# A fused attention and two-layer gate kernel: the first four layer steps in two halves of 256 tokens

## The chip, the cores and the metric

The kernel runs on one core of one Trainium2 chip. The metric is the device time of one launch in microseconds (us); lower is better. Before the change the median of three runs is 987.04 us (983.0 to 988.54). TensorE does the matrix products, VectorE, ScalarE and POOL (GpSimd) the elementwise work, and SP issues the DMAs.

## What is computed

A gated linear attention over 4 batches of 8 heads, 768 positions, head size 48, then two layers on the 3072 tokens of 384 features, with a hidden width of 2048:

```
for t in range(S):
    state = alpha[:, :, t, :, None] * state + einsum('bhd,bhe->bhde', k[:, :, t], v[:, :, t])
    y[:, :, t] = einsum('bhd,bhde->bhe', q[:, :, t], state)
x = y as (3072, 384)
h = x @ w_in;  P = a0 + a1 h + a2 h^2 + a3 h^3;  Q = 1 + |b0||h| + |b1| h^2
x = (P / (Q + 1e-6)) @ w_out
h = x @ w2_in;  out = (h * tanh(softplus(h))) @ w2_out
```

The layer weights come as float64. All matrix products of the layers keep more than float32r precision: each operand is split into a high and a low part.

## The kernel before, in words

The positions are cut into six blocks of 128; a block holds 4 x 128 = 512 tokens. The attention of a block (`attend`) is two units (`attn_unit`), unit 0 for batches 0 and 1, unit 1 for batches 2 and 3; unit `b` yields 256 tokens. A unit is a chain: scores (line 449), six levels of a tree (line 482), transposes of K (line 546), the state's outer products (line 561), the outputs (lines 596, 632), and for blocks 0 and 1 their transposes (line 546 again) with copies on ScalarE into `xf` (line 657).

The layers are 12 phases (`PHASES`: layer, block) of 16 steps, one step for each 128 hidden features, 192 steps in all. A step has nine hidden matmuls (`hidden_mms`, line 673: three input slices by the three products high x high, high x low, low x high) of 128x512 into one of three PSUM banks, the gate (`hidden`: lines 688 to 706 for the first layer, a Mish at line 710 for the second), a split of the gate's result into high and low part (`split_g`, through the helpers at lines 226/228 and 219/221), and nine output matmuls (`out_mms`, line 722) that add into three further banks over the whole phase. The first layer's gate is five ScalarE instructions, three or four on VectorE, and one multiplication on POOL for some blocks. The input of a phase is split into `xh` and `xl` by `split_x` (cast at line 226 or 228, subtraction on VectorE at line 667). In the first phase of each layer `load_w` turns the float64 weights into high and low parts on ScalarE and VectorE (lines 340 to 369).

The order on each engine is set ahead of time. Every piece of work is put into a `Plan` with an engine, a cost, a due time, and what it reads and writes; `Plan.order` runs a list scheduler, the ready piece with the earliest due time first, and emits all instructions in that order. Due times come from `T_PH` (one number for each phase, times 16 steps), `LAG`, `D_MID`, `D_SPL`, and for the attention from `AT_P*` and `AT_W`. Letters in strings such as `E_GH`, `E_TREE`, `E_GL1` choose an engine by block (V VectorE, A ScalarE, P POOL). VectorE instructions that read PSUM are entered with `port=False`; the others and POOL's exclude each other in the plan. Until the first full layer step the plan fills TensorE's free time with warm-up matmuls (line 766) of 128x256 that compute nothing; each is two pieces in the trace.

The attention of block 0 uses the PSUM pair `bank[0]`, `bank[1]` for unit 0 and banks 2 and 3 for unit 1; block 1 uses the pair for both. The main loop before, at a phase's start:

```
split_x(l, V[i] - D_X)
if l == 0 and c < NBLK - 1:
    attend(c + 1)
```

## Time and profile before

| | |
|---|---|
| runs | 983.0, 987.04, 988.54 us; median 987.04 |
| profiled execution | 989.03 us, span of its instructions 987.2 us |
| mean granted TensorE clock | 0.997 of full speed |
| busy share | TensorE 97%, VectorE 69%, ScalarE 62%, POOL 22% |

A busy share is a mean over stages; the table of stretches shows them apart. Idle time of an engine is split by what ended it ("<- DVE zp L699": a VectorE instruction of line 699 that wrote zp). PEld is TensorE's weight load, which overlaps its matmuls. A matmul's duration in the trace overlaps the next one's; the distance of two starts is what it takes.

### The profile page before, as it was taken

To read this page: it belongs to the slowest core of one execution; us is meant where nothing else is said; L and a number is where in the kernel's file an instruction comes from. 1 tells how busy PE (TensorE), PEld (TensorE's weight loads), DVE (VectorE), ACT (ScalarE), POOL (GpSimd) and SP (SyncE) were. 2 spreads that over 40 slices of the span, in tenths; PEclk is the share of its full clock that TensorE was granted. 3 is DMA by queue.
4 is the path that set the end of the run, shared out by engine and by line. 5 is a ranking of instruction groups with operands and counts; after the bars stand their busy time and mean duration, and the time that the engine had idled before them with its cause. 6 is when DMAs were issued, how large, how long until landed. Compare 5 with 4: busy or idle time off the path is not lost.

```text
span 987.2 us, 24492 instructions
## 1 busy us (share of the span) xinstructions
PE 957.1 (97%) x10370; PEld 779.8 (79%) x10370; DVE 680.8 (69%) x907; ACT 610.4 (62%) x1042; POOL 219.5 (22%) x172
## 2 busy tenths in 40 slices
PE   7988998999999999999999999999999999999998
PEld 6776876778878888888878778888888878888886
DVE  5879899989999999927796985449921288611100
ACT  2787989799966688621488633457721398723422
POOL 2034575534200000233323200000023200000232
PEclk9999999999999999999999999999999999999999
DMA  7474848774688898469636856465565555565531
GB/s 307 137 258 195 277 134 304 248 242 145 238 325 311 277 326 288 139 203 309 220 85 210 280 201 205 124 190 148 146 207 155 154 156 148 164 191 145 162 105 46
DMA packets 75757, 199.99 MB, mean 203 GB/s; under 512 B 8192, under 2 KB 34944, under 8 KB 74112
## 3 DMA queue, kind: packets, MB, share of 16 engines
q1 hardware_dynamic: 75648, 198.43, 61.8%
q8 instruction: 81, 1.33, 0.5%
q14 instruction: 28, 0.23, 0.1%
...
## 4 chain that ended last, share of the span: by engine, by line
PE 69%; DVE 8%; ACT 4%; DMA 2%; issue 1%; POOL 0%; DVEq 0%; SPq 0%
PE bank L722 33%; PE bank L673 31%; PE pair L482 3%; DVE zp L706 1%; PE pair L632 1%; DMA qka<-in_qka_dram 1%; DVE zp L697 1%; DVE zp L699 1%; DMA stage<-in_w2o_dram 1%; PE pair L546 1%; PE pair L561 1%; ACT zp L701 1%; DVE stage L345 1%; DVE qka L497 1%; ACT u L688 1%
## 5 line engine op out<-in xcount | busy, mean ns | idle before, releaser
L722 PE MATMUL bank<-gg,wo 128*128 128x512 f32 x1728 | 428.1, 393 | 1.4 <-DVE wo L219 0.7
L722 PEld LDWEIGHTS bank<-gg,wo 128*128 128x128 f32 x1728 | 322.1, 188 | 69.6 <-DVE wo L219 1.1
L673 PE MATMUL bank<-xh,wih 128*128 128x512 f32 x576 | 229.3, 398 | 3.0 <-DVE zp L699 2.5
L673 PE MATMUL bank<-xl,wih 128*128 128x512 f32 x576 | 225.2, 391 | 1.3 <-DVE xl L667 1.3
L673 PE MATMUL bank<-xh,wl 128*128 128x512 f32 x576 | 225.0, 391 | 0.0
L221 POOL TENSOR_TENSOR gg<-zp,gg 128x512 fp32r<-128x512 f32 x64 | 92.2, 1441 | 399.9 <-DVE gg L228 205.4
L710 ACT ACTIVATE zp<-bank 128x512 f32<-128x512 f32 x96 | 57.2, 597 | 168.6 <-PE bank L673 151.9
L219 DVE TENSOR_TENSOR gg<-zp,gg 128x512 fp32r<-128x512 f32 x128 | 89.3, 703 | 71.7 <-ACT gg L226 71.3
L673 PEld LDWEIGHTS bank<-xh,wih 128*128 128x128 f32 x576 | 108.3, 188 | 27.4 <-DVE zp L699 3.9
L673 PEld LDWEIGHTS bank<-xl,wih 128*128 128x128 f32 x576 | 108.4, 188 | 23.3 <-DVE xl L667 2.0
L673 PEld LDWEIGHTS bank<-xh,wl 128*128 128x128 f32 x576 | 108.3, 188 | 22.8
L226 ACT CAST gg<-zp 128x512 fp32r<-128x512 f32 x144 | 89.4, 621 | 59.4 <-PE bank L722 42.2
L695 POOL TENSOR_TENSOR zp<-zp,u 128x512 f32<-128x512 f32 x48 | 70.1, 1463 | 111.3 <-ACT zp L694 111.1
L701 ACT ACTIVATE zp<-zp,c 128x512 f32<-128x512 f32 x96 | 69.5, 726 | 13.7 <-DVE zp L691 7.5
L697 DVE SCALAR_TENSOR_TENSOR zp<-zp,sc,bank 128x512 f32<-128x512 f32 x96 | 71.0, 742 | 9.3 <-ACT zp L696 8.9
L688 ACT ACTIVATE u<-bank 128x512 f32<-128x512 f32 x96 | 57.2, 596 | 27.0 <-PE bank L673 24.0
L699 DVE SCALAR_TENSOR_TENSOR zp<-zp,sc,bank 128x512 f32<-128x512 f32 x96 | 71.3, 744 | 2.9 <-ACT u L688 1.3
L570 POOL TENSOR_TENSOR tmp<-X,qk 48x768 f32<-48x768 f32 x16 | 26.1, 1629 | 197.5 <-DVE X L575 148.0
L696 ACT ACTIVATE zp<-bank,sc 128x512 f32<-128x512 f32 x96 | 66.4, 691 | 4.6 <-PE bank L673 4.5
L706 DVE SCALAR_TENSOR_TENSOR zp<-zp,sc 128x512 f32<-128x512 f32 x80 | 63.9, 804 | 7.4 <-ACT zp L705 5.6
L482 PEld LDWEIGHTS pair<-qka 48*64 48x64 f32 (+4 forms) x3200 | 45.1, 126 | 28.5 <-issue 10.6
L733 DVE COPY u<-bank 128x512 f32<-128x512 f32 x12 | 8.3, 692 | 82.9 <-PE bank L722 82.9
...
## 6 DMA issues: line engine op xcount, KB each, us to landing
wo<-woD SPq DMA_DIRECT2D x160, 384.0 KB, 3.3
wl<-wlD SPq DMA_DIRECT2D x160, 192.0 KB, 2.5
...
```

Source lines behind the costliest of these rows:

```text
L219: dve(n, due, reads, writes, lambda: nc.vector.tensor_tensor(**kw()))
L221: pool(n, due, reads, writes, lambda: nc.gpsimd.tensor_tensor(**kw()))
L226: act(n, due, reads, writes, lambda: nc.scalar.copy(out=out(), in_=in_()), src="s")
L482: nc.tensor.matmul(bk[j][o:o + m, lo + 32 * g:lo + 32 * (g + 1)].rearrange("p (n l) -> p n l", l=L), lhsT=K[h, e * HC:e * HC + m], rhs=Qv[ ...
L673: nc.tensor.matmul(bank[hb], lhsT=w[:, k * P:(k + 1) * P], rhs=x[k], start=(k == 0 and j == 0), stop=(k == KT - 1 and j == 2))
L688: act(NTOK, due, [kh, "tab"], [ku], lambda: nc.scalar.activation(u, h, AF.Abs), table="ln")
L695: pool(NTOK, due, [ku], [kz], lambda: nc.gpsimd.tensor_tensor(out=zs[r], in0=zs[r], in1=u, op=ALU.mult))
L697: dve(NTOK, due, [kh], [kp], lambda: nc.vector.scalar_tensor_tensor(out=ps[r], in0=ps[r], scalar=A2, in1=h, op0=ALU.add, op1=ALU.mult), po ...
L699: dve(NTOK, due, [kh], [kp], lambda: nc.vector.scalar_tensor_tensor(out=ps[r], in0=ps[r], scalar=A1, in1=h, op0=ALU.add, op1=ALU.mult), po ...
L701: act(NTOK, due, [], [kz], lambda: nc.scalar.activation(zs[r], zs[r], AF.Ln, bias=c_1), src="s", ptr=1, table="ln")
L706: dve(NTOK, due, [kw], [kp], lambda: nc.vector.scalar_tensor_tensor(out=ps[r], in0=ps[r], scalar=A0, in1=w(), op0=ALU.add, op1=ALU.mult), ...
L722: nc.tensor.matmul(bank[5 + k], lhsT=wos[b][:, w, k * P:(k + 1) * P], rhs=x[q], start=(f == 0 and j == 0), stop=(f == FT - 1 and j == 2))
```

## The change

The first four steps of the first phase are made in two halves of 256 tokens, as 128x256 matmuls. The first half (`h = 0`) needs unit 0's tokens alone; its hidden products go to the pair's banks and its gate buffers lie in `xf` and `q1`, which nothing else uses then. The second half uses the usual buffers. The order in the program is first halves, then `attend(1)`, then second halves. The input of the first phase is not copied to `xf`: ScalarE rounds it from PSUM to `xh`, and VectorE subtracts from PSUM to `xl`. Further: the gate's cast in the first phase moves from ScalarE to VectorE (`E_GH`); Mish results of blocks 1, 4 and 5 stay in their PSUM bank, from where they are split (`R_MISH`); the tree of block 5 and a product of block 4 go from VectorE to POOL; all due times have new values, with an offset for each weight load (`Q_CV`) and each half step (`Q_H`, `Q_HO`). The new letters B and C of the weight conversion are not used in `E_CV`, and the strings `E_YC`, `E_XH`, `E_KC` say ScalarE throughout.

```diff
-E_GH = ('AAAAVA', 'AVAVAA')
+E_GH = ('VAAAVA', 'AVVAAA')
-T_PH = (8.402, 4.739, 4.796, 8.179, 6.234, 8.56, 2.241, 9.509, 5.286, 22.879, 7.86, 1.937)
+T_PH = (10.073, 5.514, 5.295, 4.65, 6.569, 12.843, 1.516, 12.633, 0.776, 22.477, 6.651, 4.257)
-AT_W = ((-0.128, 67.387), (21.099, 31.988), (11.236, 69.526))
+AT_W = ((-6.443, 95.112), (37.494, 62.046), (-0.915, 14.198))
+NH = 4
+Q_H = (-1.546, -3.174, 20.938, 9.585, -64.563, -53.758, 42.057, -18.307)
+Q_HO = (-21.147, -10.271)
+HB = (0, 1)
-E_TREE = 'PPPVVV'
-E_QK = 'VVVVVV'
+E_TREE = 'PPPVVP'
+E_QK = 'VVVVPV'
-E_GL1 = 'VPVPVP'
+E_GL1 = 'VPVPPV'
+R_MISH = '.G..GG'
...
-        pe(0.6, now(), [kv], kB, lambda: transposes(vn, KT), 0.5)
+        for ds in ((0,), (1,)) if c == 0 else ((0, 1),):
+            pe(0.3 * len(ds), now(), [kv] + [kv + "ab"[d] for d in ds], [kB[d] for d in ds], lambda ds=ds: rows(ds), 0.5)
...
+                evict(E_XH[b][d], DM, now(), [kB[d]], ["xhb" + x], lambda t=t, y=y: xha[:, :, t], lambda y=y: y)
+                dve(DM, now(), [kB[d], "xhb" + x], ["xlb" + x], lambda t=t, y=y: nc.vector.tensor_tensor(
+                    out=xla[:, :, t], in0=y, in1=xha[:, :, t].bitcast(F32), op=ALU.subtract), port=False)
...
+    def gate_bufs(r, j, h2):
+        if h2:
+            n = NTOK if h2 == 2 else NTOK // 2
+            return zs[r][:, 0:n], ps[r][:, 0:n], us[j][:, 0:n], ""
+        n = NTOK // 2
+        t = [x[:, y * n:(y + 1) * n] for x in (xf.rearrange("p k t -> p (k t)"), q1.rearrange("p a d -> p (a d)")) for y in range(6)]
+        return t[r], t[NZ + r], t[2 * NZ + j], "h"
...
-            act(NTOK, due, [kh] + ([] if last else ["tab"]), [kp] + (["tab"] if last else []),
-                lambda: nc.scalar.activation(ps[r], h, AF.Mish), table="mish")
+            ko, o = (kh, h) if R_MISH[c] == "G" else (kp, pr)
+            act(n, due, [kh] + ([] if last else ["tab"]), [ko] + (["tab"] if last else []),
+                lambda: nc.scalar.activation(o, h, AF.Mish), table="mish")
...
+        if in_bank:
+            dve(n, due, [kp, kgh], [kgl], lambda: nc.vector.tensor_tensor(
+                out=gl, in0=g, in1=gh.bitcast(F32), op=ALU.subtract), port=False)
...
+        n, cs = (NTOK, slice(0, NTOK)) if h == 2 else (NTOK // 2, slice(h * NTOK // 2, (h + 1) * NTOK // 2))
+
         def mms(k):
             for j, (w, x) in enumerate(((0, ghs), (0, gls), (1, ghs))):
-                nc.tensor.matmul(bank[5 + k], lhsT=wos[b][:, w, k * P:(k + 1) * P], rhs=x[q],
-                                 start=(f == 0 and j == 0), stop=(f == FT - 1 and j == 2))
+                nc.tensor.matmul(bank[5 + k][:, cs], lhsT=wos[b][:, w, k * P:(k + 1) * P], rhs=x[q][:, 0:n],
+                                 start=(f == 0 and j == 0 and h != 1), stop=(f == FT - 1 and j == 2), skip_group_check=open_)
...
+    def step(i, hb, a, b, t, to, h=2):
+        l, _, f = steps[i]
+        r, q = count[0] % NZ, count[0] % NG
+        hidden_mms(hb, l, f, a, t, h)
+        count[0] += 1
+        hidden(l, hb, r, i, t + D_MID, h)
+        split_g(l, r, q, hb, i, t + D_MID + D_SPL[l], h)
+        out_mms(f, q, b, to, h, i < FT)
+
+    def half_step(i, h):
+        a, b = slots[i - i % 2]
+        t = V[i] + Q_H[h * NH + i]
+        step(i, HB[i % 2] if h == 0 else 2 + i % 2, a + i % 2, b + i % 2, t, t + LAG[0] + Q_HO[h], h)
...
-            split_x(l, V[i] - D_X)
-            if l == 0 and c < NBLK - 1:
+            if i:
+                split_x(l, V[i] - D_X)
+            if i == 0:
+                for h in range(2):
+                    for g in range(NH):
+                        half_step(g, h)
+                    if h == 0:
+                        hand_over(lent)
+                        attend(1)
+            elif l == 0 and c < NBLK - 1:
                 attend(c + 1)
```

The order of TensorE behind unit 0's output transposes (`pair<-cst,vn`), before. L365/L366 make low parts of weights, L766 is warm-up, `bank<-cst,zp` are the K transposes of unit 1:

```order
L546 MATMUL pair<-cst,vn_141 128x128 x6
L365 MATMUL bank_125<-stage,cst 128x384
L366 MATMUL bank_125<-wih_2_73,minus 128x384
L766 MATMUL bank_124<-cst 128x256 x3
L546 MATMUL bank_122<-cst,zp 128x128 x4
L546 MATMUL bank_123<-cst,zp 128x128 x4
L766 MATMUL bank_124<-cst 128x256 x4
```

And with the change (lines 390/391, 571, 684, 714 and 838 are what 365/366, 546, 546, 673 and 766 were):

```order
L684 MATMUL pair<-cst,vn_137 128x128 x6
L390 MATMUL bank_123<-stage,cst 128x384
L391 MATMUL bank_123<-wih_2_73,minus 128x384
L714 MATMUL pair<-xh,wih_0_71 128x256
L714 MATMUL pair<-xl,wih_0_71 128x256
L714 MATMUL pair<-xh,wl_87 128x256
```

Hidden matmuls of half width (128x256) stand where warm-up stood; twelve more like the last three rows follow before unit 1's K transposes.

The order of TensorE at unit 1's output transposes (`bank<-cst,u`), before, where the row of 128x512 is the first of the layers; `pair<-qka` is attention block 1:

```order
L766 MATMUL bank_124<-cst 128x256
L482 MATMUL pair<-qka_140 64x32 x32
L546 MATMUL bank_122<-cst,u 128x128 x3
L546 MATMUL bank_123<-cst,u 128x128 x3
L766 MATMUL bank_124<-cst 128x256 x5
L482 MATMUL pair<-qka_140 60x32 x32
L673 MATMUL bank_122<-xh_102,wih_0_71 128x512
L673 MATMUL bank_122<-xl_105,wih_0_71 128x512
L673 MATMUL bank_122<-xh_102,wl_87 128x512
```

With the change, where L794 is an output matmul (722 before) and L474 (449 before) is the first of attention block 1:

```order
L794 MATMUL bank_122<-gg,wo_91 128x256 x3
L794 MATMUL bank_123<-gg,wo_91 128x256 x3
L838 MATMUL bank_120<-cst 128x256
L684 MATMUL bank_118<-cst,u 128x128 x3
L684 MATMUL bank_119<-cst,u 128x128 x3
L838 MATMUL bank_120<-cst 128x256
L474 MATMUL pair<-qka_136 64x64 x32
L714 MATMUL bank_118<-xh,wih_0_71 128x256
L714 MATMUL bank_118<-xl,wih_0_71 128x256
L714 MATMUL bank_118<-xh,wl_87 128x256
```

Output matmuls of first halves stand ahead of unit 1's transposes, and block 1's attention has moved behind them.

The order of VectorE around unit 1's state (`X_137`), before; L228 with `xh` and L667 make the first input:

```order
L575 TENSOR_TENSOR X_137<-tmp,bank_122 48x8x48
L575 TENSOR_TENSOR X_137<-tmp,bank_123 48x8x48
L517 COPY_PREDICATED AT_139<-cst,pair 128x512
L491 TENSOR_TENSOR qka_140<-qka_140 128x1024
L219 TENSOR_TENSOR wo_94<-stage,wo_94 128x2x384
L357 SCALAR_TENSOR_TENSOR stage<-stage 128x768
L517 COPY_PREDICATED AT_139<-cst,pair 128x256x2
L497 TENSOR_TENSOR qka_140<-qka_140 128x2x256x2
L228 CAST xh_102<-xf 128x512
L228 CAST xh_103<-xf 128x512
L667 TENSOR_TENSOR xl_105<-xf,xh_102 128x512
L667 TENSOR_TENSOR xl_106<-xf,xh_103 128x512
```

With the change, from unit 0's input on (L696); L748, L750 and L759 are the gate (697, 699, 706 before), L600 is the state, L382, L243 and L234 are weights (357, 228, 219):

```order
L696 TENSOR_TENSOR xl<-pair,xh 128x3x128 x2
L748 SCALAR_TENSOR_TENSOR xf<-xf,sc,pair 128x256
L750 SCALAR_TENSOR_TENSOR xf<-xf,sc,pair 128x256
L382 SCALAR_TENSOR_TENSOR stage<-stage 128x768
L243 CAST wo_94<-stage 128x2x384
L234 TENSOR_TENSOR wo_94<-stage,wo_94 128x2x384
L759 SCALAR_TENSOR_TENSOR xf<-xf,sc,pair 128x256
L748 SCALAR_TENSOR_TENSOR xf<-xf,sc,pair 128x256
L243 CAST gg<-xf 128x256
L750 SCALAR_TENSOR_TENSOR xf<-xf,sc,pair 128x256
L759 SCALAR_TENSOR_TENSOR xf<-xf,sc,pair 128x256
L243 CAST gg<-xf 128x256
```

Gate instructions of the first halves now stand ahead of unit 1's state, and block 1's work (L517, L491, L497) is no longer there.

## Rows read from the trace of the kernel before

**Rows 1.** Page, part 1: busy us (share of the span) and instructions, TensorE.
```profile
PE 957.1 (97%) x10370; PEld 779.8 (79%) x10370; DVE 680.8 (69%) x907; ACT 610.4 (62%) x1042; POOL 219.5 (22%) x172
```

**Rows 2.** Busy us of each engine (instructions) by stretch; granted clock, DMA share, GB/s.
```profile
54.43:77.98 23.55, 20.44 (x481) 16.86 (x479) 16.60 (x21) 17.95 (x29) 9.11 (x8) 1.00 0.82 289
77.98:100.00 22.02, 18.73 (x259) 14.66 (x257) 20.36 (x23) 17.16 (x31) 11.07 (x7) 0.92 0.42 158
100.00:160.00 60.00, 58.65 (x912) 46.93 (x911) 54.54 (x59) 55.76 (x92) 37.45 (x29) 1.00 0.64 219
160.00:205.00 45.00, 41.03 (x654) 31.91 (x653) 42.66 (x52) 37.81 (x76) 23.05 (x18) 1.00 0.78 268
205.00:500.00 295.00, 294.10 (x3219) 239.30 (x3218) 256.56 (x340) 197.63 (x339) 64.04 (x45) 1.00 0.74 248
500.00:600.00 100.00, 96.29 (x1253) 78.41 (x1244) 83.88 (x111) 66.78 (x117) 22.55 (x17) 1.00 0.64 209
600.00:983.60 383.60, 381.87 (x2461) 315.08 (x2459) 167.16 (x255) 188.01 (x315) 43.05 (x33) 1.00 0.51 150
```

**Rows 3.** The same view for line 766 alone, the warm-up matmuls.
```profile
54.43:77.98 23.55, 9.93 (x40) 7.19 (x40) 1.00 0.82 289
```

**Rows 4.** Timeline of TensorE at 793 us: start, us, what, [idle before <- releaser].
```profile
793.55 0.51 PE L673 MATMUL bank<-xh,wih 128*128 128x512 f32 x1 [1.51 <-DVE zp L699]
```

**Rows 5.** Timeline of TensorE at 92 us.
```profile
92.13 0.76 PE L482 MATMUL pair<-qka 48*32 48x32 f32 x64 [1.96 <-DVE zp L706]
92.81 3.35 PE L722 MATMUL bank<-gg,wo 128*128 128x512 f32 x9
95.96 0.63 PE L673 MATMUL bank<-xh,wih 128*128 128x512 f32 x1
96.39 0.63 PE L673 MATMUL bank<-xl,wih 128*128 128x512 f32 x1
```

**Rows 6.** Chain that ended last, at 387 us: start, us, what.
```profile
386.96 2.04 PE bank L722 x9
```

**Rows 7.** Timeline of TensorE, 62 to 79 us.
```profile
62.30 1.12 PE L449 MATMUL pair<-qka 48*64 48x64 f32 x63
...
75.58 0.97 PE L482 MATMUL pair<-qka 48*60 48x32 f32 x54
...
77.98 0.50 PE L673 MATMUL bank<-xh,wih 128*128 128x512 f32 x1
```

**Rows 8.** Groups by line and shape, ScalarE: count | busy us, mean ns | idle before.
```profile
L688 ACT ACTIVATE u<-bank 128x512 f32<-128x512 f32 x96 | 57.2, 596 | 27.0 <-PE bank L673 24.0 <-DMA out_dram<-u 1.1 <-DVE zp L697 1.0
...
L694 ACT ACTIVATE zp<-u,sc 128x512 f32<-128x512 f32 x48 | 39.0, 817 | 0.1
```

**Rows 9.** Timeline of ScalarE, 70 to 74 us.
```profile
71.02 0.86 ACT L653 COPY u<-bank 128x384 f32<-128x384 f32 x2 [2.42 <-PE bank L596]
...
73.31 0.86 ACT L657 COPY xf<-bank 128x384 f32<-128x384 f32 x2
```

**Rows 10.** Timeline of VectorE at 170 us.
```profile
170.39 1.89 DVE L667 TENSOR_TENSOR xl<-xf,xh 128x512 fp32r<-128x512 f32 x3
```

**Rows 11.** Groups by line and shape, VectorE.
```profile
L219 DVE TENSOR_TENSOR gg<-zp,gg 128x512 fp32r<-128x512 f32 x128 | 89.3, 703 | 71.7 <-ACT gg L226 71.3
...
L228 DVE CAST gg<-zp 128x512 fp32r<-128x512 f32 x48 | 20.7, 433 | 60.8 <-ACT zp L710 51.7 <-PE bank L722 8.9
```

**Rows 12.** Timeline of TensorE, 200 to 210 us.
```profile
203.22 1.09 PE L546 MATMUL pair<-cst,qka 128*128 128x128 f32 x8
204.07 0.47 PE L673 MATMUL bank<-xh,wih 128*128 128x512 f32 x1
```

**Rows 13.** Groups by line and shape, TensorE weight loads.
```profile
L673 PEld LDWEIGHTS bank<-xl,wih 128*128 128x128 f32 x576 | 108.4, 188 | 23.3 <-DVE xl L667 2.0
```

**Rows 14.** TensorE's waits, 500 to 600 us: us in total, times, longest.
```profile
PE bank L673 <- DVE xl L667: 1.3, 1, 1.3
PE bank L673 <- DVE zp L699: 1.0, 1, 1.0
```

More of the change, by code (lines that the diff above doesn't have):

```diff
@@ L204, in pe @@
     def pe(us, due, reads, writes, emit, rows=1.0):
-        plan.add("PE", us if us == 0.680 else us + 0.2, due, reads, writes, emit, after=rows)
+        plan.add("PE", us if us in (0.680, 0.360) else us + 0.2, due, reads, writes, emit, after=rows)
     def dve(n, due, reads, writes, emit, port=True, fast=False, ptr=0):
@@ L214, in pool, with evict @@
         plan.add("POOL", 0.15 + (0.0021 if n > 2 * P else 0.00254) * n, due, reads, writes, emit, True)
+    def evict(eng, n, due, reads, writes, out, in_):
+        if eng == "A":
+            act(n, due, reads, writes, lambda: nc.scalar.copy(out=out(), in_=in_()))
+        else:
+            dve(n, due, reads, writes, lambda: nc.vector.tensor_copy(out=out(), in_=in_()), port=False)
     def tt(eng, n, due, reads, writes, kw):
@@ L679, in hidden @@
-    def hidden(l, hb, r, i, due):
+            pe(0.680 if h == 2 else 0.360, due, [f"wih{l}_{f // 2}", f"wl{a}"] + [f"xh{k}", f"xl{k}"] + xb, [f"bank{hb}"], lambda k=k: mms(k))
+    def gate_bufs(r, j, h2):
[5 more added lines that the diff above has]
+        return t[r], t[NZ + r], t[2 * NZ + j], "h"
@@ new lines, in hidden @@
+            kw = kh if R_PSUM[c] in "RG" else kz
+            w = lambda: h if R_PSUM[c] in "RG" else zr
+            ko = kh if R_PSUM[c] == "G" else kp
+            o = lambda: h if R_PSUM[c] == "G" else pr
+            act(n, due, [kz], [kw] + (["tab"] if last else []),
+                lambda: nc.scalar.activation(w(), zr, AF.Exp, scale=-1.0), src="s", table="ln")
+            dve(n, due, [kw, kp], [ko], lambda: nc.vector.scalar_tensor_tensor(
+                out=o(), in0=pr, scalar=A0, in1=w(), op0=ALU.add, op1=ALU.mult), port=R_PSUM[c] not in "RG", ptr=1)
+        else:
+            ko, o = (kh, h) if R_MISH[c] == "G" else (kp, pr)
+            act(n, due, [kh] + ([] if last else ["tab"]), [ko] + (["tab"] if last else []),
+                lambda: nc.scalar.activation(o, h, AF.Mish), table="mish")
```

143 lines of the change are left out of this document (88 added, 55 removed).

## Prediction

> **What bounds the kernel now.** I read the page's busy shares first, then busy times by stage, then TensorE's timeline and waits in the stages that are not full. TensorE is busy 97% of the span [rows 1], so the time is TensorE's useful work plus what it loses. From 205 us to 500 us it idles 0.9 us in 295 [rows 2]: there nothing is to be won. The losses lie in three places. From 54.43 to 77.98 us (the first attention unit, "unit 0", is through and the second, "unit 1", is not) it idles 3.1 us, and 9.9 us of its busy time are warm-up matmuls that compute nothing [rows 2, 3]. From 77.98 to 100 us, the pipe's first fill, it idles 3.3 us, and from 100 to 205 us 5.3 us [rows 2]. From 500 to 600 us it idles 3.7 us, and a wait of 1.5 us stands at 793 us [rows 2, 4]. A loss that is not idle time: from 92.81 us, after an idle of 1.96 us, nine output matmuls took 3.15 us up to the next start where nine take 2.04 us elsewhere, and the three hidden ones behind them start 0.43 us apart instead of 2.04 / 9 = 0.227 [rows 5, 6]; the granted clock of that stage is 0.92 on average [rows 2]. That is 1.1 + 3 x 0.2 = 1.7 us. VectorE stands close behind: 91% busy from 100 to 160 us, 95% from 160 to 205 us [rows 2].
>
> **The change part by part.** All sums start from the profiled execution: 989.03 us, of which 987.2 us are span; that is 2.0 us above the median of the three runs, 987.04 us, and I carry the difference over to the median.
>
> *Half steps in place of warm-up.* In the new order 54 half matmuls (36 hidden, 18 output) stand ahead of unit 1's transposes, and 7 warm-up matmuls instead of 20 stand behind unit 0's. Useful work brought forward: 54 halves are 27 full ones at 0.227 us, 6.1 us. The 13 warm-up matmuls that go are 13 x 9.93 / 20 = 6.5 us (each is two of the 40 pieces of [rows 3]), so there is room for it without a later start. On the other side, four TensorE groups of attention block 1 began before the first layer matmul at 77.98 us, from 62.30 to 75.58 us (the first and the last of the four are in [rows 7]); now one does. Three groups of about 1.12 us, 3.4 us, come later. Net 2.7 us won.
>
> *Unit 1's chain and its input.* ScalarE gets 20 half-width activations of the first half's gates, and they stand between the copies of unit 1 that TensorE waits for: three ahead of its K copies, five ahead of its state copies, the rest ahead of its output copies. Half of the shortest and of the longest of the full-width ones is 0.30 and 0.41 us [rows 8]; I take 0.35. The first eight make unit 1 some 3 us late; the rest fall for the most part into the 2.42 us that ScalarE waited for TensorE before 71.02 us [rows 9]. Ends 0 and 5. Against this the input is rounded from PSUM: before, from the copies into xf to the first matmul it took 77.98 - 73.31 = 4.7 us [rows 7, 9], with rounding and subtraction on VectorE in between; now two casts and two subtractions of 384 columns, about 2.0 us: the two copies of that width took 0.86 us, and a subtraction of 512 columns 0.63 us in a row of three, so 0.55 us each is on the safe side [rows 9, 10]. That gives 2.7 us back. Net 0.3 us lost, taken as 0: the second halves start near 78 us, as the first full steps did.
>
> *The fill, 78 to 100 us.* Outputs of the first halves are then ready while the second halves are still in the gates, so TensorE has work where it waited: 3.3 us of idle and 1.7 us of low clock. I take 3.5 of these 5.0 us; ends 0 and 5.0. From 100 to 205 us I take 1.3 of 5.3 us, for VectorE sets the pace there.
>
> *VectorE's load.* E_GH moves the cast of the first phase from ScalarE to VectorE: 16 x 0.43 us (the casts' mean [rows 11]), 6.9 us more, in a stretch where VectorE is 91 to 95% busy. Up to the last input subtraction of block 1 the new VectorE order holds 31 gate instructions more, 24 of the new ones of half width, some 8 us at 0.2 to 0.7 us each by the same rows, and four weight conversions more; TensorE's order is then 1.33 groups of nine further, 2.7 us. VectorE idled 14.1 us from 54.43 to 160 us [rows 2], which covers it if half of that can be used. I charge 2.0 us; ends 0 and 8.
>
> *Halves cost more than wholes.* 144 half matmuls stand for 72 full ones. No row shows 256 columns in this format. Below: exactly half, 0.113 us, no cost. Above: no gain from the narrower operand, 0.227 us, 16.3 us. The nearest row: eight 128-column transposes with the same 128x128 float32 weights follow each other in 0.85 us, 0.106 us each [rows 12], so the array takes new weights at least that fast, though a single load reads 188 ns [rows 13]. I take 0.12 us: 144 x 0.12 - 16.3 = 0.9 us lost. The Trainium skill, "TensorE: Matmul & The Clock Gate", section "LDWEIGHTS (loading the stationary operand)", has a load of 128 columns take 128 / 1.2 = 107 ns however wide the moving operand is, which at 256 columns is as long as the matmul itself. By that rule an estimate of 144 x 0.109 us gives a gain of 0.6 us instead of the loss, and the row of 0.106 us agrees with it better than the one of 188 ns does.
>
> *Later parts.* Block 4's attention is due over 95 us instead of 67, block 5's over 62 instead of 32 (AT_W), and one product of block 4 and the tree of block 5 go to POOL, which is 23% busy there. The idle of 500 to 600 us and the wait at 793 us end mostly on VectorE instructions [rows 14], an engine that is 84% busy from 500 to 600 us [rows 2]; spread thinner, I take half of 3.7 + 1.5 us, 2.6 us; ends 0 and 5.2. Mish results that stay in PSUM (blocks 1, 4, 5) move 32 subtractions from POOL to VectorE at 0.70 us each [rows 11]: 11 us of block 1's come between 205 and 500 us, where VectorE has 38 us of room and covers them, the others behind 600 us, where it is 44% busy [rows 2]. I cost it at nothing; without that cover it would be up to 11 us.
>
> Sum: 2.7 + 0 + 3.5 + 1.3 - 2.0 - 0.9 + 2.6 = 7.2 us. 989.0 - 7.2 = 981.8 us for the profiled execution, 987.0 - 7.2 = **979.8 us** for the median.
>
> **The rivals.**
> *All waits go.* The whole of 5.0, 5.3 and 5.2 us is recovered and neither VectorE nor the halves cost: 2.7 + 5.0 + 5.3 + 5.2 = 18.2, 969 us. For it: the idle before 205 us has many small causes that one order can avoid. Against: VectorE at 95%.
> *VectorE gives it back.* The 6.9 us of casts and the earlier gates meet a VectorE that has no room, and the 2.7 + 3.5 + 1.3 us shrink to 2 while the late 2.6 us stay away: with the halves' 0.9 us, 986 us. For it: 91 to 95% busy. Against: its 8.6 us of idle from 54.43 to 100 us fall in the stretch that gets the new work [rows 2].
> *Weight loads set the halves' pace.* At 0.188 us per half matmul [rows 13], 90 of the 144 (those that do not stand in place of warm-up) cost 0.075 us more each, 6.8 us: 979.8 + 6.8 = 986.6 us. For it: the row. Against: the 0.106 us of the transposes.
> *The clock falls.* With 12 fewer warm-up matmuls in all, the thin stretch of 55 to 78 us may fall to the lower of TensorE's levels (1.2 against 2.4 GHz). Each stretch like that at 92.81 us costs 1.7 us; two of them make it 983.2 us. The Trainium skill, "TensorE: Matmul & The Clock Gate", section "HAM oscillation — how this bites in real kernels", warns that idle gaps bring the lower clock back; by that rule taking out filler work is a risk, and the stage at 0.92 agrees with it.
> *Slower: block 1's attention comes too late.* Its first matmuls ran at 62.30 us [rows 7]; now they stand behind unit 1's transposes, some 11 us later, on the same PSUM pair that the first halves' gates read. Its input split was through at 172.3 us [rows 10]. If the lateness is not made up, the second phase starts up to 11 us late with 2.7 us of other work to cover it: 8.3 us lost and 0.9 for the halves, the gains before that gone, the late 2.6 kept: 987.0 + 6.6 = 993.6 us. For it: VectorE's fuller order. Against: its idle 14.1 us. It decides from where the last input subtraction of block 1 ends later than about 175 us.
> That the half steps do not come forward at all can be excluded: the order of TensorE's instructions is fixed, and they stand ahead of unit 1's.
>
> **How the numbers follow.** A measurement of this kernel can tell about 0.5%, 4.9 us, from no change, so faster means under 982.1 us. Forecast 0.53, with its own range of 974 to 984 us; most of it (0.46) lies under 982.1. All waits go 0.11. VectorE gives it back 0.13, loads 0.05, clock 0.05: within 0.5%. Block 1 too late 0.13. So faster 0.57, same 0.30, slower 0.13. The range leaves out half of the best case and the slower one: 970 to 989 us.
>
> **What would show it.** Warm-up matmuls behind unit 0 take about 3.5 us instead of 9.9. The first half-width hidden matmul starts near 57 us, the second halves near 78 us, at 0.12 us from one to the next. TensorE's idle time from 78 to 100 us falls to about 1 us and no stretch there reads under 0.95 in clock. The last input subtraction of block 1 ends before 175 us. Idle time from 500 to 600 us is about 2 us. It would be wrong with: half matmuls at 0.19 us or more; idle from 100 to 205 us above 5 us with VectorE as releaser; unit 1's transposes behind 78 us.

## The result, and the profile after

The changed kernel takes **996.5 us** (median of 4 runs, 995.88 to 999.33) against 985.92 us of the kernel before on the same chip: a ratio of 1.0114, 95% interval 1.0077 to 1.0150. It is about 11 us slower. The forecast was 979.8 us, the range 970 to 989. Below, a ratio's distance from 1 is turned into time with 986 us, the median of the kernel before. Every experiment had runs of the kernel before beside it, whose medians lay between 985.45 and 987.78 us, so ratios are compared and not bare medians. A difference of two ratios carries the uncertainty of both, some 4 us here. Line numbers of the changed kernel: hidden products L714, outputs of the layers L794, gate L739 to L759, levels L507, scores L474, output transposes L684, subtractions of the split input L705 (L696 for block 0).

The busy times of the profiled execution (999.33 us, span 997.5 us), first from part 1 of the page, then by the stretches of [rows 2], in the same columns:

```profile
PE 959.8 (96%) x10418; PEld 783.4 (79%) x10418; DVE 699.5 (70%) x954; ACT 607.4 (61%) x1047; POOL 180.1 (18%) x162
```

```profile
54.43:77.98 23.55, 19.03 (x282) 15.38 (x282) 12.04 (x22) 17.55 (x35) 5.85 (x7) 0.88 0.40 124
77.98:100.00 22.02, 21.09 (x398) 18.15 (x399) 21.63 (x36) 15.69 (x33) 12.18 (x15) 1.00 0.75 301
100.00:160.00 60.00, 52.07 (x860) 41.49 (x852) 58.67 (x72) 50.01 (x80) 38.35 (x29) 0.93 0.66 225
160.00:205.00 45.00, 36.56 (x625) 28.83 (x625) 37.67 (x46) 32.18 (x66) 16.91 (x16) 0.90 0.69 233
205.00:500.00 295.00, 292.99 (x3130) 237.28 (x3131) 256.59 (x350) 194.15 (x335) 38.43 (x29) 1.00 0.73 248
500.00:600.00 100.00, 99.73 (x1519) 82.12 (x1518) 91.17 (x112) 74.11 (x129) 37.74 (x32) 1.00 0.63 205
600.00:983.60 383.60, 382.72 (x2466) 315.89 (x2465) 182.18 (x271) 191.11 (x321) 22.09 (x17) 1.00 0.53 156
```

The fill from 78 to 100 us is as good as forecast: TensorE idles 0.9 us instead of 3.3. The late stretch is better than forecast: 0.3 us of idle from 500 to 600 us instead of 3.7. The loss lies from 100 to 205 us: 7.9 + 8.4 = 16.4 us of idle where [rows 2] have 5.3, with the granted clock at 0.93 and 0.90 where it was 1.00.

TensorE's timeline of the changed kernel, first around the half steps and the start of block 1's attention, then around its last levels:

```profile
55.04 0.80 PE L507 MATMUL bank<-zp 48*32 48x32 f32 x42 [3.23 <-issue]
...
59.41 0.55 PE L714 MATMUL pair<-xh,wih 128*128 128x256 f32 x1 [0.50 <-DVE xl L696]
...
79.25 0.92 PE L684 MATMUL bank<-cst,u 128*128 128x128 f32 x6
...
80.82 1.16 PE L474 MATMUL pair<-qka 48*64 48x64 f32 x64 [0.22 <-DVE q L759]
81.91 0.38 PE L714 MATMUL bank<-xh,wih 128*128 128x256 f32 x1
...
82.25 0.28 PE L714 MATMUL bank<-xh,wl 128*128 128x256 f32 x1
...
83.92 0.28 PE L714 MATMUL bank<-xl,wih 128*128 128x256 f32 x1
...
103.28 0.92 PE L507 MATMUL pair<-qka 48*48 48x32 f32 x64 [2.72 <-DVE AT L542]
105.09 0.80 PE L714 MATMUL bank<-xh,wih 128*128 128x512 f32 x1 [0.89 <-DVE zp L759]
105.69 0.63 PE L714 MATMUL bank<-xl,wih 128*128 128x512 f32 x1
...
108.67 0.63 PE L714 MATMUL bank<-xh,wl 128*128 128x512 f32 x1
...
160.17 1.50 PE L507 MATMUL pair<-qka 48*48 48x32 f32 x64 [3.44 <-DVE qka L522]
164.94 1.08 PE L507 MATMUL pair<-qka 48*32 48x32 f32 x64 [3.26 <-ACT AT L537]
```

Three things are to be seen. Half matmuls follow each other in (83.92 - 82.25) / 14 = 0.119 us. Block 1's scores start at 80.82 us where they started at 62.30 [rows 7], and the row names what let them go: a gate instruction of a first half (`q` is one of its lent buffers, L759), which reads the pair bank that the scores write. TensorE waited only 0.22 us for it; nearly all of the delay is the place that the plan gave to the scores, behind the first halves and unit 1's transposes. From 103 us on TensorE stands in front of block 1's levels and waits for that chain; after the wait of 2.72 us the hidden matmuls start (108.67 - 105.69) / 7 = 0.426 us apart, the pace of [rows 5].

VectorE's timeline, the last subtraction of block 1's input, which [rows 10] have at 170.39 us:

```profile
187.07 1.90 DVE L705 TENSOR_TENSOR xl<-xf,xh 128x512 fp32r<-128x512 f32 x3 [0.93 <-ACT xh L241]
```

It ends at 188.97 us, 16.7 us later than before (172.28). What that costs is shown by the work of the layers that TensorE had done by then. Groups of TensorE by line and shape, first the kernel before from 54 to 172.3 us, then the changed one from 54 to 189 us (of the hidden matmuls one of three products each; the other two have the same counts):

```profile
L673 PE MATMUL bank<-xh,wih 128*128 128x512 f32 x50 | 20.9, 417 | 0.4 <-DVE zp L706 0.4
...
L722 PE MATMUL bank<-gg,wo 128*128 128x512 f32 x129 | 35.1, 409 | 1.2 <-DVE wo L219 0.7 <-POOL gg L221 0.4
```

```profile
L794 PE MATMUL bank<-gg,wo 128*128 128x512 f32 x105 | 27.1, 397 | 0.6 <-POOL gg L236 0.6
...
L714 PE MATMUL bank<-xh,wih 128*128 128x512 f32 x38 | 17.8, 469 | 1.7 <-DVE zp L759 1.3 <-ACT xh L241 0.2
...
L794 PE MATMUL bank<-gg,wo 128*128 128x256 f32 x72 | 10.7, 289 | 0.0
...
L714 PE MATMUL pair<-xh,wih 128*128 128x256 f32 x12 | 4.2, 348 | 3.6 <-ACT q L747 0.9 <-ACT q L739 0.8 <-DVE xf L748 0.8
L714 PE MATMUL bank<-xh,wih 128*128 128x256 f32 x12 | 3.6, 299 | 0.0
```

Sixteen steps have 48 such hidden matmuls. Before it is 50 at that moment, now 38 + 24 / 2 = 50: in both kernels the hidden products of all sixteen steps of block 0 are out, with six of the nine of the next step. Of block 0's 144 output matmuls 129 were out before and 105 + 72 / 2 = 141 are now: twelve more, 12 x 0.227 = 2.7 us of work, filled part of the 16.7 us. When block 1's input is late, this is all that TensorE has left of the layers to put in its place.

### The profile page after: what moved, and what is told of

The parts are those of the page before. It is cut to its first block, busy times and chain, and to the rows that moved or that the text cites. A ratio compares the mean times of both kernels' runs of the same rounds, so it can differ in the third digit from the quotient of the medians.

```text
span 997.5 us, 24570 instructions
## 1 busy us (share of the span) xinstructions
PE 959.8 (96%) x10418; PEld 783.4 (79%) x10418; DVE 699.5 (70%) x954; ACT 607.4 (61%) x1047; POOL 180.1 (18%) x162
## 4 chain that ended last, share of the span: by engine, by line
PE 84%; DVE 5%; ACT 5%; DMA 3%; issue 2%; POOL 0%; SPq 0%; ACTq 0%; DVEq 0%; POOLq 0%
PE bank L794 37%; PE bank L714 37%; PE pair L507 4%; PE pair L657 2%; PE bank L838 2%; DVE qka L522 1%; PE pair L571 1%; PE pair L586 1%; DMA stage<-in_w1o_dram 1%; DMA qk<-in_nat_dram 1%; DMA x2d<-u 1%; DMA stage<-in_w2o_dram 1%; DVE zp L750 1%; ACT stage L378 1%; ACT stage L357 0%
## 5 line engine op out<-in xcount | busy, mean ns | idle before, releaser
L794 PE MATMUL bank<-gg,wo 128*128 128x512 f32 (+1 forms) x1764 | 428.6, 388 | 0.6 <-POOL gg L236 0.6
L794 PEld LDWEIGHTS bank<-gg,wo 128*128 128x128 f32 x1764 | 323.8, 188 | 68.1 <-POOL gg L236 1.2
L714 PE MATMUL bank<-xh,wih 128*128 128x512 f32 (+1 forms) x576 | 229.4, 398 | 4.4 <-ACT u L739 2.7
L714 PE MATMUL bank<-xl,wih 128*128 128x512 f32 (+1 forms) x576 | 224.6, 390 | 0.2 <-DVE xl L705 0.2
L714 PE MATMUL bank<-xh,wl 128*128 128x512 f32 (+1 forms) x576 | 224.5, 390 | 0.0
L714 PEld LDWEIGHTS bank<-xh,wih 128*128 128x128 f32 x576 | 108.8, 189 | 29.3 <-ACT u L739 3.5
L714 PEld LDWEIGHTS bank<-xh,wl 128*128 128x128 f32 x576 | 109.0, 189 | 22.9 <-DVE wl L234 0.2
L714 PEld LDWEIGHTS bank<-xl,wih 128*128 128x128 f32 x576 | 109.1, 189 | 21.4 <-DVE xl L705 0.5
L783 DVE TENSOR_TENSOR gg<-bank,gg 128x512 fp32r<-128x512 f32 x48 | 33.2, 691 | 97.6 <-ACT gg L777 97.2
L748 DVE SCALAR_TENSOR_TENSOR zp<-zp,sc,bank 128x512 f32<-128x512 f32 (+1 forms) x96 | 70.0, 731 | 24.1 <-ACT zp L747 23.5
L746 POOL TENSOR_TENSOR zp<-zp,u 128x512 f32<-128x512 f32 (+1 forms) x48 | 65.0, 1359 | 119.7 <-ACT zp L745 119.2
L752 ACT ACTIVATE zp<-zp,c 128x512 f32<-128x512 f32 (+1 forms) x96 | 68.6, 717 | 23.3 <-DVE zp L742 15.1
L234 DVE TENSOR_TENSOR gg<-zp,gg 128x512 fp32r<-128x512 f32 x112 | 76.9, 691 | 4.3 <-ACT gg L241 3.6
L750 DVE SCALAR_TENSOR_TENSOR zp<-zp,sc,bank 128x512 f32<-128x512 f32 (+1 forms) x96 | 70.2, 733 | 1.9
L507 PEld LDWEIGHTS pair<-qka 48*64 48x64 f32 (+4 forms) x3200 | 46.1, 128 | 30.6 <-issue 9.8
L236 POOL TENSOR_TENSOR gg<-zp,gg 128x512 fp32r<-128x512 f32 (+1 forms) x32 | 43.7, 1369 | 141.3 <-ACT gg L241 108.0
L759 DVE SCALAR_TENSOR_TENSOR zp<-zp,sc 128x512 f32<-128x512 f32 x80 | 64.3, 813 | 5.5 <-ACT zp L758 2.8
L747 ACT ACTIVATE zp<-bank,sc 128x512 f32<-128x512 f32 (+1 forms) x96 | 65.2, 679 | 4.5 <-PE bank L714 4.4
```

What stands on the lines that cost most here:

```text
L234: dve(n, due, reads, writes, lambda: nc.vector.tensor_tensor(**kw()))
L507: nc.tensor.matmul(bk[j][o:o + m, lo + 32 * g:lo + 32 * (g + 1)].rearrange("p (n l) -> p n l", l=L), lhsT=K[h, e * HC:e * HC + m], rhs=Qv[ ...
L714: nc.tensor.matmul(bank[hb][:, 0:n], lhsT=w[:, k * P:(k + 1) * P], rhs=x[k][:, cs], start=(k == 0 and j == 0), stop=(k == KT - 1 and j == 2))
L746: pool(n, due, [ku], [kz], lambda: nc.gpsimd.tensor_tensor(out=zr, in0=zr, in1=u, op=ALU.mult))
L747: act(n, due, [kh], [kp], lambda: nc.scalar.activation(pr, h, AF.Copy, scale=A3), ptr=1)
L748: dve(n, due, [kh], [kp], lambda: nc.vector.scalar_tensor_tensor(out=pr, in0=pr, scalar=A2, in1=h, op0=ALU.add, op1=ALU.mult), port=False, ...
```

## The experiments

Sixteen kernels ran beside the kernel before. "Ready" is the start of the last subtraction of block 1's input, "scores" that of block 1's first scores, both from the timelines.

| kernel | ratio to before (95%) | scores, us | ready, us |
|---|---|---|---|
| the changed kernel | 1.0114 (1.0077 to 1.0150) | 80.8 | 187.1 |
| e1 full first steps | 1.0278 (1.0243 to 1.0313) | 62.6 | 184.8 |
| e2 casts on ScalarE | 1.0213 (1.0165 to 1.0261) | 81.3 | 191.8 |
| e3 late load | 1.0108 (1.0073 to 1.0142) | 80.2 | 185.0 |
| e4 old late parts | 1.0216 (1.0177 to 1.0255) | 80.7 | 185.5 |
| e5 old early due times | 1.0312 (1.0258 to 1.0366) | 84.5 | 197.9 |
| e6 full, old due, new late | 1.0074 (1.0048 to 1.0099) | 63.0 | 170.0 |
| e7 rounding from PSUM alone | 1.0037 (1.0013 to 1.0062) | 61.7 | 168.5 |
| e8 less VectorE | 1.0075 (1.0048 to 1.0102) | 80.9 | 182.5 |
| e9 two half steps | 1.0198 (1.0166 to 1.0231) | 73.4 | 185.5 |
| e10 attention late, alone | 1.0165 (1.0132 to 1.0199) | 76.1 | 185.6 |
| e11 halves in bank 4 | 1.0257 (1.0221 to 1.0294) | 65.2 | 183.0 |
| e12 the same, old tables | 1.0232 (1.0197 to 1.0266) | 66.7 | 182.1 |
| e13 attention less late | 1.0093 (1.0059 to 1.0127) | 71.0 | 177.3 |
| e14 before, all late parts | 0.9961 (0.9939 to 0.9983) | 62.9 | 168.8 |
| e15 before, late letters | 0.9988 (0.9967 to 1.0009) | 62.7 | 171.2 |
| e16 before, late times | 0.9981 (0.9963 to 0.9998) | 62.0 | 167.9 |

### One part undone at a time

```diff
e1  -NH = 4
    +NH = 0
```

> Edit: NH is 0, so that block 0's first four steps run on 512 tokens behind both units, as before the change; the rounding from PSUM and all the new due times stay. Theory A (the half steps hold block 1's attention back: they use the pair banks and bring VectorE 6.9 us of casts while VectorE is busy 9.4 to 10.0 of every 10 us from 80 to 170 us): block 1's first scores come back to some 62 us from 80.8, its last rounding of the input ends before 180 us (187 to 189 in the changed kernel), the idle of 0.89, 2.72, 3.44 and 3.26 us at 99 to 163 us goes for the most part, the stall of 3.2 us at 52 us too, and the time is 985 us or less, 11 below the changed kernel. Theory B (the new due times order block 1's levels badly, whatever the steps are): the waits at 155 to 163 us stay and the time is 992 to 998 us.

Measured 1013.69 us. The scores came back to 62.6 us, as theory A said, but the input was ready no sooner than 184.8 us, and the time is 16 us above the changed kernel. Both theories fall as they stood: with the new tables the full steps are slower than the halves, and an early start alone does not make the chain end early.

```diff
e2  -E_GH = ('VAAAVA', 'AVVAAA')
    +E_GH = ('AAAAVA', 'AVVAAA')
```

> Edit: the first letter of E_GH[0] is A again, so the casts gh of block 0 in layer 1 (8 of 256 and 12 of 512 elements, about 6.9 us by rows of 0.23 to 0.45 us) go from VectorE to ScalarE; the halves stay. Theory A1 (VectorE's sum sets the pace from 80 to 170 us, and each us taken off it comes back): the waits of TensorE on VectorE at 99 to 160 us shrink by 5 us or more and the time is 988 to 992 us. Theory A2 (the order of block 1's attention behind the first halves costs the time, not the casts): 995 us or more, with the waits moved to ScalarE, which is itself busy 8 of 10 us there.

Measured 1006.34 us, by its time A2's side and 10 us worse than the changed kernel: within these tables the casts are better placed on VectorE. The waits did not move to ScalarE, as A2 had it; TensorE's long ones from 99 to 163 us still end on VectorE.

```diff
e3  -dma(1573, now() - 8, [], [kQC, kK, kal], ...)
    +dma(1573, due(0.5) - 5 if u == 2 else now() - 8, ["xhb0"] if u == 2 else [], [kQC, kK, kal], ...)
```

> Edit: on SyncE's queue the load of block 1's Q, K and gates (1.5 MB) changes places with the load of block 1's values behind it, which waits for unit 0's transposes; so it starts near 57.6 us in place of 50.3, and all other orders stay. Theory C (the stall of 3.2 us at 52 us comes because the fetch of TensorE's next instructions lies in a stretch where this load fills the DMA queues): the stall falls below 1 us, the clock of 52 to 60 us rises over 0.9, and the time falls by 3 to 5 us, to 992 to 993.5 us. Rival (what is won at 52 us is waited off again by 160 us, since VectorE, full from 80 to 170 us, sets the pace): the stall falls, and the time stays at 995.5 to 997.5 us. Rival 2 (the fetch is slow of itself): the stall stays at 3 us.

Measured 996.85 us. Windows of 52 to 56 and 56 to 60 us (columns as in the table of stretches) and TensorE's waits from 50 to 60 us, first the changed kernel:

```profile
52.00:56.00 4.00, 0.96 (x43) 0.90 (x43) 1.25 (x3) 1.37 (x3) 0.00 (x0) 0.64 1.02 370
56.00:60.00 4.00, 3.50 (x12) 2.39 (x12) 2.12 (x3) 2.65 (x6) 0.00 (x0) 0.50 0.70 223
```

```profile
PE bank L507 <- issue: 3.2, 1, 3.2
```

then this run:

```profile
52.00:56.00 4.00, 1.59 (x46) 1.52 (x46) 1.28 (x2) 0.74 (x1) 0.00 (x0) 0.56 0.14 55
56.00:60.00 4.00, 3.50 (x15) 2.40 (x14) 1.49 (x3) 3.27 (x7) 0.00 (x0) 0.58 0.58 178
```

```profile
PE bank L507 <- issue: 3.2, 1, 3.2
```

The DMA share of the first window fell from 1.02 to 0.14 and the stall stayed 3.2 us, which is the outcome of rival 2; theory C is false. What TensorE waits for there no row names, so that it is a fetch of instructions is not shown. The stall goes with the half steps: the nine kernels that have them (the changed one, e2 to e5, e8, e9, e11, e12) all show it at this group of L507, 3.1 to 4.9 us long, and the nine without (the kernel before among them) show no idle time of this kind from 40 to 64 us.

```diff
e4  AT_W, AT_P, E_TREE, E_QK, R_MISH, E_GL1, E_GH[1], T_PH[4:] as before the change
e5  T_PH[:4], AT_P1, Q_CV, X_LEAD, D_X, E_HC as before the change
```

> Edit: the changed kernel with the parts that act behind the fourth phase as before (AT_W, AT_P, E_TREE, E_QK, R_MISH, E_GL1, E_GH of layer 2, the last eight of T_PH); the halves, the rounding from PSUM and the new early due times stay. Theory D (the late parts gain some 5 us, since TensorE's idle of 500 to 600 us fell from 3.7 to 0.3 us and the wait at 800 us from 1.5 to 0.65): idle of over 3 us at 500 to 600 us is back, and the time is 1000 to 1003 us. Rival (the late waits only show what the late start had already cost: with block 1 behind by 10 us, later work is never short of inputs): no idle comes back, and the time stays within 1.5 us of 996.5 us.

Measured 1007.84 us, theory D's side and 4.8 us over its range: behind the changed early part the late parts are worth 1.0216 - 1.0114, 10 us. The idle is back, 3.0 us at 500 to 600 us and 3.7 us at 300 to 400 us; the stretches of this run:

```profile
300.00:400.00 100.00, 96.34 (x1133) 77.38 (x1132) 91.29 (x124) 73.66 (x124) 5.13 (x3) 0.98 0.87 298
500.00:600.00 100.00, 97.00 (x1381) 79.55 (x1380) 91.07 (x124) 74.88 (x129) 37.40 (x22) 0.98 0.66 213
```

> Edit: the changed kernel, halves and late parts as they are, with the early due times as before (the first four of T_PH, AT_P1, Q_CV all zero, X_LEAD, D_X, E_HC). Theory B1 (the new early due times alone make the waits of 99 to 163 us): those waits fall below 4 us together and the time is 983 to 988 us. Theory B2 (halves and due times were set to each other, and either alone is worse than both, as the full steps with the new due times were at 1013.7): 1000 us or more.

Measured 1018.33 us, B2. With the late parts new, the four combinations (of which the first, e6 below, also has the casts on ScalarE) of halves (no, yes) and early times (old, new) read 1.0074, 1.0278, 1.0312 and 1.0114: either alone costs 16 to 23 us more than none or both. The tables are set to each other, and a part taken alone has no price of its own.

### The starting points

```diff
e6  e5 with NH = 0 and E_GH[0] = 'AAAAVA'
e7  e6 with all late parts as before: the rounding of block 0's input from PSUM is left (with its transposes in two groups)
```

> Edit: full first steps, early due times and casts of block 0 as before; the late parts and the rounding of the first input from PSUM as in the changed kernel. Theory D (the late parts gain by themselves, and the early part loses by itself): the time is 975 to 982 us, below both kernels, since undoing the late parts cost 11 us in the run on them. Rival (the late parts gain only behind the changed early part, to whose times they are set): 984 to 990 us.

Measured 994.56 us, a miss of theory D, and 4.6 us over the upper end of the rival.

> Edit: the changed kernel's code with every table as before and full first steps; what is left of the change is that block 0's first input is rounded from PSUM by four casts of 384 elements and four subtractions, with its transposes in two groups. Theory E (the first steps start some 3 us earlier and the rest keeps its order): 982 to 984 us. Rival (the plan orders block 1's levels anew around the earlier steps, and they come later against the steps, at step 13.0 in place of 12.7 and 4.3 in place of 3.0): 986 to 992 us.

Measured 990.19 us, the rival's side: the kernel loses 1.3 to 6.1 us, with the input of block 1 ready 1.9 us sooner than before. The rounding itself does what it was to do; the first hidden matmul came at 73.84 us instead of 77.98:

```profile
73.84 0.47 PE L714 MATMUL bank<-xh,wih 128*128 128x512 f32 x1
```

By the stretches there is a loss further back:

```profile
100.00:160.00 60.00, 55.80 (x837) 43.71 (x835) 56.95 (x61) 55.18 (x89) 39.02 (x29) 1.00 0.66 222
160.00:205.00 45.00, 42.00 (x636) 33.52 (x637) 38.90 (x49) 34.90 (x72) 17.23 (x16) 0.85 0.72 245
```

TensorE idles 4.2 us from 100 to 160 us (1.3 in [rows 2]) and has a clock of 0.85 from 160 to 205 us. That the plan's other order of block 1's levels does this was not tried apart from the rounding. An earlier start of the layer steps was not a gain here.

### Is it VectorE's sum?

```diff
e8  -dve(n, due, [kh], [kp], lambda: nc.vector.scalar_tensor_tensor(
    +dve(n, due, [kh], [kp], lambda: None if c == 0 else nc.vector.scalar_tensor_tensor(
         out=pr, in0=pr, scalar=A1, in1=h, op0=ALU.add, op1=ALU.mult), ...)
```

> Left out of the computation: block 0's second step of the polynomial in layer 1 (the instruction with A1, 8 of 256 and 12 of 512 elements on VectorE, 12.8 us by their rows of 0.48 and 0.74 us); every queue keeps its order otherwise. Theory F (VectorE's sum, 9.4 to 10.0 us of every 10 from 80 to 170 us, sets the pace of the changed kernel there): TensorE's waits at 99 to 163 us fall by half or more, the clock stays over 0.95, and the time falls by 8 us or more, to 988 us or less. Rival (single late hand-overs in an order that the plan fixed set the pace, and VectorE is busy only because it works ahead): 993 us or more.

Measured 993.66 us, a fall of 1.0114 - 1.0075, some 4 us and by the intervals not clear of zero, for 12.8 us taken off VectorE. The rival's side. From 100 to 160 us VectorE is still busy 56.18 of 60 us and TensorE idles 9.2:

```profile
100.00:160.00 60.00, 50.81 (x918) 40.85 (x909) 56.18 (x66) 50.20 (x82) 42.15 (x30) 0.97 0.66 225
```

The input of block 1 is ready 4.5 us sooner, and the time falls by about as much. So VectorE's load does not act as a sum; that it acts through the chain's end fits, but rests on this one run.

### The start of block 1's attention alone

```diff
e10 -pe(1.3, now(), [kK, kQC], kB, scores_0, 0.5)
    +pe(1.3, now(), [kK, kQC] + ["xlb3"] * (u == 2), kB, scores_0, 0.5)
e13 the same with "v1a" in place of "xlb3"; both on the kernel of e7
```

> Edit: the kernel of the run with the rounding from PSUM alone (990.2 us, no halves, all times and late parts as before the change), with one dependency added for the plan: block 1's first scores stand behind the rounding of unit 1's half of the input, so that they come near 74 us in place of 61.7. Theory G: block 1's input is ready some 10 to 12 us later, near 181 us in place of 169.8, and the time rises by 6 to 12 us, to 996 to 1002 us. Rival (the layer steps move up into the gap, and nothing is lost): 990 to 993 us.

> Edit: as in the run that delayed block 1's attention alone, but with its first scores behind the copy of unit 1's outputs, so that they come near 70 to 72 us (61.7 without a delay, 76.1 in that run). Theory G1 (every us of delay costs about one): block 1's input is ready near 179 us, and the time is 997 to 1001 us. Theory G2 (there is cover until some 175 us and the loss begins behind it): 991 to 996 us.

Measured 1003.85 and 996.95 us, against 990.19 without the delay. The two rows of each run, scores from TensorE's timeline and the last subtraction from VectorE's; without the delay (e7):

```profile
61.68 1.16 PE L474 MATMUL pair<-qka 48*64 48x64 f32 x64
...
168.54 2.58 DVE L705 TENSOR_TENSOR xl<-xf,xh 128x512 fp32r<-128x512 f32 x3 [0.31 <-ACT xh L241]
```

e13:

```profile
70.98 1.16 PE L474 MATMUL pair<-qka 48*64 48x64 f32 x64
...
177.28 1.88 DVE L705 TENSOR_TENSOR xl<-xf,xh 128x512 fp32r<-128x512 f32 x3
```

e10:

```profile
76.11 1.16 PE L474 MATMUL pair<-qka 48*64 48x64 f32 x64
...
185.61 1.90 DVE L705 TENSOR_TENSOR xl<-xf,xh 128x512 fp32r<-128x512 f32 x3 [0.26 <-ACT xh L241]
```

The last subtraction ends at 171.12, 179.16 and 187.51 us. By the ratios 8.0 us of lateness cost 5.5 us (1.0093 - 1.0037) and 16.4 us cost 12.6 (1.0165 - 1.0037), each within some 4 us. Part of the lateness was covered. The output matmuls of block 0 that were out by then, from 54 us on, in e7, e13 and e10:

```profile
L794 PE MATMUL bank<-gg,wo 128*128 128x512 f32 x129 | 34.5, 410 | 0.0
```

```profile
L794 PE MATMUL bank<-gg,wo 128*128 128x512 f32 x144 | 36.4, 395 | 0.0
```

```profile
L794 PE MATMUL bank<-gg,wo 128*128 128x512 f32 x144 | 39.5, 410 | 0.8 <-DVE wo L234 0.8
```

All 144 were through in the delayed kernels, 15 more than in e7, which is 15 x 0.227 = 3.4 us of work put in between. Lateness less this cover is 4.6 and 13.0 us, beside 5.5 and 12.6 measured. Behind the cover a late microsecond costs about a whole one, as far as two runs with this uncertainty can tell. Theory G of e10 has the sign right, with a time 1.9 us over its range; e13's 996.95 us lies between the ranges of G1 and G2 and does not decide between them. Nothing but the start of the chain was asked for here, but the plan moved other pieces with it: the first full hidden matmul came at 76.65 us (e13) and 77.21 us (e10) instead of 73.84. Still, e10 makes a kernel without any half steps nearly as slow as the changed kernel with the old late parts (e4), 1.0165 against 1.0216.

### Can the start be kept and the halves too?

```diff
e9  -NH = 4                    +NH = 2
e11 -HB = (0, 1)               +HB = (8, 9)   (the two halves of bank 4; no warm-up once they begin)
e12 e11 with every table and letter as before the change
```

> Edit: NH is 2, so that only the first two layer steps run in halves; due offsets of those as in the changed kernel. The pair banks are then used once each by first halves. Theory G (the start of block 1's attention sets when its input is ready, and so the time): first scores near 70 to 73 us in place of 80.8, last subtraction of block 1's input near 177 us in place of 187, and the time is 988 to 993 us. Rival (the tables were set for four half steps, and any other number disturbs the order): 998 us or more, though the scores come sooner.

> Edit: the changed kernel with the four first halves in the two halves of bank 4 in place of the pair banks, and no warm-up matmuls after the first of them (they write bank 4). Theory G: block 1's first scores come near 63 us, its input is ready near 172 us, and the time falls by 8 us or more, to 988 us or less. Rival (the halves' gates and the due times hold the attention back as much as the banks): scores at 63 us, input ready after 180 us, and 993 us or more.

> Edit: the halves in bank 4 as in the run before this, with every due time, engine letter and late part as before the change (only the halves and the rounding from PSUM stay). Theory G: scores near 63 us, input ready near 172 us or sooner, and the time is that of the rounding from PSUM alone or better, 983 to 990 us. Rival (the halves lose by themselves, whatever bank and tables they have): 995 us or more.

Measured 1006.2, 1011.74 and 1009.91 us, the rivals' side in all three. In e11 the other bank let the scores start 15.6 us sooner than in the changed kernel, and the timelines show that this was not enough:

```profile
65.19 1.16 PE L475 MATMUL pair<-qka 48*64 48x64 f32 x64
...
122.67 1.16 PE L475 MATMUL pair<-qka 48*64 48x64 f32 x64
...
182.99 1.89 DVE L706 TENSOR_TENSOR xl<-xf,xh 128x512 fp32r<-128x512 f32 x3
```

From the scores to that subtraction it takes 117.8 us, against 106.3 in the changed kernel and 108.1 before. When the chain starts early beside the halves, it is longer by most of what it gained; e1, with no halves but the new early times, has 122.2 us. The second row is the first of block 1's second unit; in e7 it reads

```profile
118.03 1.16 PE L474 MATMUL pair<-qka 48*64 48x64 f32 x64
```

From there to the last subtraction it takes 50.5 us in e7 and 50.7 in the changed kernel (from 136.42 us), but 60.3 in e11, 61.3 in e1 and 59.6 in e12. The stretch lies in the second unit, and so for the most part behind the last half-width matmul, which ends near 130 us in e11. What makes it was not settled.

### The late parts on the kernel before

```diff
e14 the kernel before with e4's list as in the change
e15 of that only R_MISH, E_GL1, E_GH[1]
e16 of that only AT_W, AT_P, E_TREE, E_QK, T_PH[4:]
```

> Edit: the kernel before, with its own first steps, first input and early due times, and all late parts of the change (AT_W, AT_P, E_TREE, E_QK, R_MISH, E_GL1, E_GH of layer 2, the last eight of T_PH). Theory D (the late parts gain by themselves, 3 to 5 us by the idle before of 3.7 us at 500 to 600 us and 1.5 us near 793 us): 980 to 983 us, below both kernels. Theory D2 (they gain only behind the early part they were set with; with the rounding from PSUM they lost 4.4 us): 988 to 992 us.

> Edit: the kernel before with the engine letters of layer 2 alone from the change (R_MISH, E_GL1, E_GH of layer 2). Theory D: part of the gain, 982 to 986 us. Theory D2 (the order that the plan makes is set anew by any letter, and the due times were set for the old ones): 988 us or more.

> Edit: the kernel before with the late due times and the attention's letters alone from the change (AT_W, AT_P, E_TREE, E_QK, the last eight of T_PH), layer 2's letters as before. Theory D: part of the gain, 982 to 986 us. Theory D2: 988 us or more, since the due times were set for the new letters.

Measured 984.99, 985.98 and 984.97 us beside 987.78 for the kernel before. e14 is the one version that beats both kernels, by 1.7 to 6.0 us against the kernel before; e15 cannot be told from the kernel before, and e16 only just. Its stretch from 500 to 600 us:

```profile
500.00:600.00 100.00, 98.64 (x1632) 80.48 (x1632) 89.33 (x112) 62.45 (x109) 36.27 (x28) 1.00 0.65 215
```

Idle 1.4 us instead of 3.7. Theory D has the sign right; its 980 to 983 us hold by the ratio (986 x 0.9961 = 982.2), not by the median. VectorE is busier there than before, 89.3 us instead of 83.9.

## Why the prediction was wrong

**The step that failed** is in the first term, "half steps in place of warm-up": "Three groups of about 1.12 us, 3.4 us, come later. Net 2.7 us won." The three groups were priced as TensorE's busy time. They are the head of a chain: block 1's two units run one after the other, some 107 us from the first scores to the last subtraction, and the second phase of the layers starts at its end. Their delay should have been priced by the chain's end: the scores started 18.5 us later (80.82 instead of 62.30), the chain took about as long as before (106.3 instead of 108.1 us), and its end came 16.7 us later, of which 14.0 us are left when the cover of 2.7 us is taken off. Where the term has 2.7 us won, the runs show that loss. The rival "block 1's attention comes too late" had this mechanism, named the pair's banks and gave 993.6 us, but a chance of 0.13. Its cover of 2.7 us was right, the twelve output matmuls; its lateness was not, 16.7 us and not 11. With 16.7 its own sum gives 987.0 + 14.0 + 0.9 - 2.6 = 999.3 us.

**Why VectorE's idle 14.1 us were no argument against it.** Idle time of an engine ahead of a chain's start cannot be used by that chain, and 7.0 of the 14.1 us lie before 77.98 us. From 54.43 to 77.98 us VectorE is busy 12.0 us in the changed kernel where it was 16.6 [rows 2]: the change added idle there.

**The other terms.** *Halves at 0.12 us*: right, 0.119; the estimated gain of 0.6 us beside it did not come. *Warm-up*: right, the windows of its line read

```profile
54.43:77.98 23.55, 2.75 (x10) 1.73 (x10) 0.88 0.40 124
```

against 9.93 us [rows 3]. The clock of that stretch fell to 0.88, as the rival "the clock falls" had it, but not where warm-up is missing: it is low in and behind the stall of 3.23 us (the windows beside e3) and then full, with little warm-up:

```profile
60.00:77.98 17.98, 14.57 (x230) 12.09 (x230) 9.79 (x19) 14.89 (x30) 5.85 (x7) 1.00 0.28 75
```

*First half near 57 us*: 59.41, behind a stall of 3.23 us that TensorE did not have in one piece before. *Unit 1's chain*, net 0, with the second halves near 78 us: mis-sized, 81.91. The transposes of unit 1 came at 79.25 us; before they stood at

```profile
72.61 0.87 PE L546 MATMUL bank<-cst,u 128*128 128x128 f32 x6
```

so the unit was 6.6 us late where some 3 us were taken. *Input from PSUM*, 2.0 us instead of 4.7: right, 81.91 - 79.83 = 2.1 us from the casts (79.83 us on ScalarE) to the first matmul, but an earlier first matmul did not make e7 faster. *Fill*: right, idle 0.9 us and clock 1.00. *100 to 205 us*, 1.3 of 5.3 us saved: idle rose by 11.1 us, the failed step seen from the other end. Two of the three signs that were to count against the forecast came: unit 1's transposes behind 78 us, and idle above 5 us from 100 to 205 us with VectorE as the main releaser. *VectorE's casts*, 2.0 us charged: by e2 leaving them on ScalarE would have cost 10 us in these tables. *Later parts*, 2.6 us: on the kernel before they gain 1.7 to 6.0 us (e14), so the size is right, but not the reason: VectorE is not spread thinner from 500 to 600 us, it is busy 91.2 us there instead of 83.9. Behind the changed early part they gain 10 us (e4), with e6's early part they lose some 4 us, barely clear of noise (1.0074 against 1.0037 in e7).

**How it adds up.** In the profiled executions block 1's input is through 16.7 us later, and from there to the end the changed kernel takes 997.5 - 188.97 = 808.5 us where the kernel before took 987.2 - 172.28 = 814.9, which is 6.4 us less. Together that is 10.3 us, the whole difference of the two spans. Of the 6.4 us, 2.7 are the cover; the other 3.7 are gained by the late parts, net of what else changed there. With the old late parts (e4) the same stretch takes 1005.4 - 187.40 = 818.0 us, so the early part also brings a loss behind the chain's end, which was not followed up.

**What stays open**: what stretches the second unit by some 10 us when the chain starts early (e1, e11, e12), so that a free bank did not bring the time back; and what TensorE's 3.2 us of "issue" are, a cost of the half steps that the prediction did not have.
